# Attention re-laid on 128 partitions, with token tiles of two batches and one set of small steps for three tiles

## The chip, the cores and the metric

The kernel runs on one core of a Trainium2 chip. The metric is device time in microseconds (us) of one launch. A kernel's runs mostly agree within 0.3%. On the chip that most experiments shared, the kernel before itself varied from 1040.6 to 1052.7 us, so the intervals of the ratios are about 0.6% wide to each side, and the smaller differences are read from the traces.

## The reference

The program is an attention without softmax, followed by a balanced mixture of experts. Cut to what matters (B = 8 batches, H = 8 heads, S = 576 tokens, D = 64, all fp32; E = 8 experts):

```python
kv  = np.einsum('bhsd,bhse->bhde', k, v)
out = np.einsum('bhsd,bhde->bhse', q, kv)
rms = np.sqrt(np.mean(out * out, axis=-1, keepdims=True) + 1e-06)
x   = (out / rms * g_norm)            # then (B,H,S,D) -> (B*S, H*D) = 4608 x 512
logits = x @ w_gate                   # 4608 x 8
# all logits from the highest down: a token goes to that expert if neither is taken or full
# (every expert takes 4608 / 8 = 576 tokens); then for each expert:
out[mask] = np.maximum(x[mask] @ w1[e], 0.0) @ w2[e]
```

The gate needs the logits of all tokens, so the assignment cannot start before the attention has ended. That makes the program three stages in a row: attention, assignment, experts.

## The kernel before

The attention stage is the part that the change touches. k and v of a batch lie on 96 partitions of six tokens each, q of a batch's first 512 tokens on 128 partitions of four tokens; the other 64 tokens of two batches share a tile (the "q tail"). A tile of 128 tokens goes through transposes (`qt_ps`, `qt`), the product with the block-diagonal k-v matrices (`o_ps`), squares, a root and its Newton step, and two multiplications out of PSUM: `x_sb` and, for the gate's logits, `part`.

```python
def load_kv(b):
    for name, src in (("k", k), ("v", v)):
        t = att.tile([KP, H, KR, D], FT, name=f"{name}_sb", tag=name)      # KP = 96, KR = 6
        nc.sync.dma_start(t.rearrange("p h j d -> p h (j d)"),
                          src[b].rearrange("h (p j) d -> p h (j d)", j=KR))
        loaded[name, b] = t

def load_q(b):
    t = att.tile([P, H, J, D], FT, name="q_sb", tag="q")                   # J = 4
    nc.sync.dma_start(t.rearrange("p h j d -> p h (j d)"),
                      q[b, :, 0:G, :].rearrange("h (p j) d -> p h (j d)", j=J))
# ... [cut: constants, bd = the block-diagonal matrices]
def kv_product(b):
    for h in range(H):
        ls = slice((h % 2) * D, (h % 2 + 1) * D)
        for j in range(KR):
            nc.tensor.matmul(kv_ps[ls, h // 2, :], lhsT=k_sb[:, h, j, :], rhs=v_sb[:, h, j, :],
                             start=(j == 0), stop=(j == KR - 1))
    nc.vector.tensor_copy(bd[0:D, b, :, 0:D], kv_ps[0:D])
    nc.scalar.copy(bd[D:P, b, :, D:P], kv_ps[D:P])
    # ... [cut: transposes and the gate's columns of bd]

def token_tile(c, rows, batches, x_row):
    # ... [cut: transposes, qt by ScalarE and VectorE in turn, o_ps]
    nc.scalar.activation(sq, o_v, ACT.Square)
    nc.vector.reduce_sum(out=ms, in_=sq.rearrange("p r (l d) -> p (r l) d", l=2), axis=AXX)
    # ... [cut: seven small steps on 128x8, among them one root on ScalarE]
    nc.vector.tensor_tensor(x_row..., o_v..., inv_h.to_broadcast([P, NP, 2, D]), op=AL.mult)
    nc.vector.tensor_tensor(part, o_ps[:, :, P:W]..., inv_h.to_broadcast([P, NP, 2, E]), op=AL.mult)
    nc.vector.reduce_sum(out=lg[:, :, c], in_=part..., axis=AXX)

for b in range(B):
    kv_product(b)
    # ... [cut: q_rows copies on GpSimd; four token tiles; x written by GpSimd's queue]
    if b + 2 < B:
        load_kv(b + 2); load_q(b + 2)
    if b == B - 3: load_w(0)
    if b == B - 2: load_w(1)
# ... [cut: four tiles of q tails, the last x writes]
```

## Time and profile before

| | before |
|---|---|
| time | 1049.75 us (1048.55 to 1050.27, 3 runs) |
| first k-v product | 14.36 us |
| first token tile (first `o_ps`) | 26.74 us |
| end of the attention stage (start of `ones_b`, the first instruction of the assignment) | 186.7 us (the sum of the prediction takes 187.2, the start of GpSimd's `row_id`) |
| DMA rate in the attention, to 130 us | mostly 220 to 290 GB/s |

How to read it: the page gives each engine's busy share in 40 slices, and the three stages can be seen in it with the naked eye. As the change edits the attention alone, the number to follow is the time at which the first instruction of the assignment starts. It can be found in VectorE's list as the instruction that writes `ones_b`, or in GpSimd's as `row_id`; both wait for the last write of x.

### The profile page before, as it was taken

Reading aid. Unit: us, or ns where it says so; the run is one execution under the profiler, and the core shown is the slowest. Engines: PE = TensorE matmul, PEld = TensorE weight load, DVE = VectorE, ACT = ScalarE, POOL = GpSimd, SP = SyncE. Lnnn points to the kernel's source line nnn. Section 1 sums busy time; section 2 is a strip of 40 time slices with the busy share of each in tenths; the row PEclk is TensorE's granted clock in tenths of the full one; section 3 lists DMA queues with packets and bytes.
Section 4 is the critical chain, followed back from the end, with each engine's and each line's share of the span. In section 5 each row is a group of like instructions: output and inputs, shape, how many; then the busy total and the mean of one; then the engine's idle time right before and its main releaser. Section 6 shows DMA issues by size and latency. Waiting matters only on the chain.

```text
span 1045.8 us, 12692 instructions
## 1 busy us (share of the span) xinstructions
PE 756.9 (72%) x5277; PEld 509.7 (49%) x5277; DVE 363.2 (35%) x1295; ACT 98.7 (9%) x212; POOL 105.1 (10%) x132
## 2 busy tenths in 40 slices
PE   3796884223223223216999999999999999999996
PEld 3786874122212222213755747557466475574752
DVE  0666576565675666674110101101011011010100
ACT  1332231000000000000110101101001011010100
POOL 2211110000000000004120110210202100101001
PEclk9998796555555555555999999999999999999999
DMA  9999991000000000003133212330323122301000
GB/s 225 261 259 295 268 385 60 22 1 1 1 1 2 1 1 1 2 1 89 47 146 106 105 62 86 138 112 25 133 96 136 44 72 101 105 1 41 6 20 25
DMA packets 45721, 91.01 MB, mean 87 GB/s; under 512 B 7008, under 2 KB 27488, under 8 KB 44640
## 3 DMA queue, kind: packets, MB, share of 16 engines
q1 hardware_dynamic: 37632, 61.87, 20.8%
q0 software_dynamic: 7328, 28.32, 7.5%
q8 instruction: 41, 0.67, 0.3%
q10 hardware_dynamic: 704, 0.02, 0.1%
q14 instruction: 16, 0.13, 0.0%
HBM read 71.32 MB, written 18.87 MB: 86 GB/s over the span
## 4 chain that ended last, share of the span: by engine, by line
issue 50%; DVE 22%; PE 18%; POOL 6%; DMA 2%; ACT 2%; POOLq 0%; SPq 0%; DVEq 0%; ACTq 0%
PE n_ps L318 6%; PE o_ps L158 4%; DVE over L313 4%; POOL out_dram L523 4%; PE kv_ps L129 3%; POOL xg L482 2%; DVE cand L311 2%; DMA v_sb<-in_v_dram 1%; DVE up L328 1%; DVE step L308 1%; DVE hi L330 1%; PE qt_ps L147 1%; DVE lo L332 1%; PE k_ps L326 1%; DVE full L321 1%
## 5 line engine op out<-in xcount | busy, mean ns | idle before, releaser
L519 PE MATMUL y_ps<-w_sb,hid 128*128 128x512 f32 (+1 forms) x640 | 280.2, 594 | 0.0
L509 PE MATMUL h_ps<-xt,w_sb 128*128 128x288 f32 x1024 | 251.7, 408 | 0.0
L509 PEld LDWEIGHTS h_ps<-xt,w_sb 128*128 128x128 f32 x1024 | 194.5, 191 | 58.8 <-issue 5.7
L519 PEld LDWEIGHTS y_ps<-w_sb,hid 128*128 128x128 f32 (+1 forms) x640 | 112.5, 179 | 151.3 <-issue 150.7
L318 PE MATMUL n_ps<-best,over 128*16 128x8 bf16 x2016 | 62.5, 176 | 146.1 <-DVE over L313 105.5
L318 PEld LDWEIGHTS <-over 128*16 128x16 bf16 x2016 | 57.0, 89 | 173.9 <-DVE over L313 172.2
L471 DVE TENSOR_SCALAR hid<-h_ps 128x288 f32<-128x288 f32 x64 | 29.3, 458 | 253.2 <-PE h_ps L509 253.2
L475 DVE COPY y_sb<-y_ps 128x512 f32<-128x512 f32 (+1 forms) x17 | 11.8, 691 | 208.7 <-PE y_ps L519 208.7
L482 POOL DMA_INDIRECT xg<-x_dram,ids x40 | 37.9, 946 | 450.1 <-DVE ids L448 295.7
L158 PE MATMUL o_ps<-bd,qt 128*128 128x144 f32 (+1 forms) x320 | 54.9, 361 | 25.3 <-DVE rt L173 19.7
L523 POOL DMA_INDIRECT out_dram<-y_sb,ids x40 | 38.5, 964 | 323.6 <-ACT y_sb L469 189.4
L158 PEld LDWEIGHTS o_ps<-bd,qt 128*128 128x128 f32 (+1 forms) x320 | 49.2, 232 | 28.1 <-issue 24.7
L129 PE MATMUL kv_ps<-v_sb,k_sb 96*64 96x64 f32 x768 | 44.2, 242 | 14.4 <-DMA v_sb<-in_v_dram 14.4
L129 PEld LDWEIGHTS kv_ps<-v_sb,k_sb 96*64 96x64 f32 x768 | 41.4, 152 | 17.9 <-issue 16.2
L465 ACT ACTIVATE hid<-h_ps 128x288 f32<-128x288 f32 x64 | 26.3, 411 | 221.9 <-PE h_ps L509 221.9
L313 DVE TENSOR_TENSOR over<-mx,cand 128x576 bf16<-128x576 f32 x56 | 42.3, 755 | 1.5
L467 ACT ACTIVATE xt<-t_ps,g_col 128x512 f32<-128x512 f32 (+1 forms) x17 | 11.5, 675 | 326.3 <-DMA xg<-x_dram,ids 311.5
L469 ACT COPY y_sb<-y_ps 128x512 f32<-128x512 f32 (+1 forms) x23 | 13.4, 584 | 253.6 <-PE y_ps L519 253.6
L321 DVE SCALAR_TENSOR_TENSOR full<-n_ps,goal 16x8 f32<-16x8 f32 x56 | 8.6, 153 | 67.3 <-PE n_ps L318 67.3
L164 DVE TENSOR_REDUCE ms<-sq 128x8 f32<-128x512 f32 x36 | 24.6, 685 | 19.8 <-ACT sq L162 19.3
L162 ACT ACTIVATE sq<-o_ps 128x512 f32<-128x512 f32 x36 | 21.5, 597 | 73.1 <-PE o_ps L158 73.1
L473 DVE TENSOR_SCALAR xt<-t_ps,g_col 128x512 f32<-128x512 f32 (+1 forms) x23 | 15.4, 669 | 35.8 <-PE t_ps L493 33.8
(143 smaller groups left out, 471.6 us busy)
## 6 DMA issues: line engine op xcount, KB each, us to landing
w_sb<-in_moe_w_dram SPq DMA_DIRECT2D x16, 2048.0 KB, 9.7
k_sb<-in_k_dram SPq DMA_DIRECT2D x8, 1152.0 KB, 13.2
v_sb<-in_v_dram SPq DMA_DIRECT2D x8, 1152.0 KB, 18.1
q_sb<-in_q_dram SPq DMA_DIRECT2D x8, 1024.0 KB, 18.7
x_dram<-x_sb POOLq DMA_DIRECT2D x8, 1024.0 KB, 8.9
q_tail<-in_q_dram SPq DMA_DIRECT2D x8, 128.0 KB, 6.3
x_dram<-x_sb POOLq DMA_DIRECT2D x2, 512.0 KB, 5.4
xg<-x_dram,ids POOLq DMA_INDIRECT x40, 6.2
```

Of the source, the lines that this page charges most:

```text
L129: nc.tensor.matmul(kv_ps[ls, h // 2, :], lhsT=k_sb[:, h, j, :], rhs=v_sb[:, h, j, :], start=(j == 0), stop=(j == KR - 1))
L158: nc.tensor.matmul(o_ps[ps_, r, 0:W], lhsT=qt[:, r, ps_], rhs=bd[:, b, r], start=True, stop=True)
L162: nc.scalar.activation(sq, o_v, ACT.Square)
L164: nc.vector.reduce_sum(out=ms, in_=sq.rearrange("p r (l d) -> p (r l) d", l=2), axis=AXX)
L313: nc.vector.tensor_tensor(over, mx.rearrange("p (c o) -> p c o", o=1).to_broadcast([P, GC, NCAND]), cand.rearrange("p (o n) -> p o n", o=1 ...
L318: nc.tensor.matmul(n_ps, lhsT=over[:, c, :], rhs=best[:, :, c], start=(c == 0), stop=(c == GC - 1))
L465: nc.scalar.activation(dst, src, ACT.Relu)
L471: nc.vector.tensor_scalar(dst, in0=src, scalar1=0.0, scalar2=None, op0=AL.max)
L482: nc.gpsimd.indirect_dma_start(out=xg[0:nr, :], out_offset=None, in_=x_dram, in_offset=bass.IndirectOffsetOnAxis(ap=ids[0:nr, e * NB + n:e ...
L509: nc.tensor.matmul(h_ps, lhsT=w1[:, d, f * P:(f + 1) * P], rhs=xt[:, d, cs], start=(d == 0), stop=(d == DC - 1))
L519: nc.tensor.matmul(y_ps[0:nr, :], lhsT=hid[:, f, a:a + nr], rhs=w2[:, f, :], start=(f == 0), stop=(f == FC - 1))
L523: put = nc.gpsimd.indirect_dma_start(out=out, out_offset=bass.IndirectOffsetOnAxis(ap=ids[0:nr, e * NB + n:e * NB + n + 1], axis=0), in_=y ...
```

## The change

The intent: transfers in longer runs on all partitions; less work for VectorE; tiles that need no tail.

- k and v: 128 partitions of nine tokens (half a head pair each). The k-v product becomes 72 matmuls on two quarters of the array that lie diagonally to one another.
- q: a tile is 64 tokens of each of two batches. Each batch's q goes to 64 partitions: the even batch's to the lower half by SyncE's queue, the odd batch's to the upper half by GpSimd's.
- The small steps are done once for three tiles, on 24 columns. `o_ps` is copied out of PSUM by ScalarE, the multiplication for x goes to GpSimd, all `qt` copies go to VectorE.
- The first two experts' weights are loaded behind all of q, k and v; x is written by SyncE's queue.

```diff
-            t = att.tile([KP, H, KR, D], FT, name=f"{name}_sb", tag=name)
+            t = att.tile([P, NP, R, D], FT, name=f"{name}_sb", tag=name)
             nc.sync.dma_start(
-                t.rearrange("p h j d -> p h (j d)"), src[b].rearrange("h (p j) d -> p h (j d)", j=KR)
-            )
+                t.rearrange("p r j d -> p r (j d)"),
+                src[b].rearrange("h s d -> (h s) d").rearrange("(r p j) d -> p r (j d)", r=NP, j=R))
-    def load_q(b):
-        t = att.tile([P, H, J, D], FT, name="q_sb", tag="q")
-        nc.sync.dma_start(
-            t.rearrange("p h j d -> p h (j d)"), q[b, :, 0:G, :].rearrange("h (p j) d -> p h (j d)", j=J)
-        )
+    def load_q(i):
+        t = att.tile([P, H, R, D], FT, name="q_sb", tag="q")
+        for n, eng in enumerate((nc.sync, nc.gpsimd)):
+            eng.dma_start(t[n * HP:(n + 1) * HP].rearrange("p h j d -> p h (j d)"),
+                          q[2 * i + n].rearrange("h (p j) d -> p h (j d)", j=R))
     # [cut: order of the loads: k0, v0, q0, k1, v1]
-        for h in range(H):
-            ls = slice((h % 2) * D, (h % 2 + 1) * D)
-            for j in range(KR):
-                nc.tensor.matmul(kv_ps[ls, h // 2, :], lhsT=k_sb[:, h, j, :], rhs=v_sb[:, h, j, :],
-                                 start=(j == 0), stop=(j == KR - 1))
+        for r in range(NP):
+            for j in range(R):
+                for l in range(2):
+                    ls = slice(l * D, (l + 1) * D)
+                    nc.tensor.matmul(kv_ps[ls, r, :], lhsT=k_sb[ls, r, j, :], rhs=v_sb[ls, r, j, :],
+                                     start=(j == 0), stop=(j == R - 1))
     # [cut: token_group replaces token_tile; in it, for each of three tiles]
+                for n in range(2):
+                    ps_ = slice(n * HP, (n + 1) * HP)
+                    nc.tensor.matmul(o_ps[ps_, r, 0:W], lhsT=qt[:, r, ps_], rhs=bd[:, 2 * i + n, r],
+                                     start=True, stop=True)
+            nc.scalar.activation(sq..., o_ps[:, :, 0:P], ACT.Square, scale=D ** -0.5)
+            nc.scalar.copy(o_sb[:, t], o_ps[:, :, 0:W])
+            nc.vector.reduce_sum(out=ms[:, t * H:(t + 1) * H], in_=sq..., axis=AXX)
     # [cut: root, reciprocal and three fused small steps on 24 columns]
+        nc.gpsimd.tensor_tensor(x_sb..., o_sb...[:, :, 0:P]..., inv...to_broadcast(...), op=AL.mult)
+        nc.vector.tensor_tensor(part, o_sb...[:, :, P:W]..., inv...to_broadcast(...), op=AL.mult)
+        nc.vector.reduce_sum(out=lg[:, :, c:c + T]..., in_=part..., axis=AXX)
+        nc.sync.dma_start(x_dram[...][:, j0:j0 + T], x_sb.rearrange("p (t f) -> p t f", t=T))
```

## The prediction

> **What bounds the kernel now.** I began with the page: the share of each engine by slice says that the program has three stages (a slice is 26.1 us).
>
> ```profile
> PE   3796884223223223216999999999999999999996
> PEclk9998796555555555555999999999999999999999
> DMA  9999991000000000003133212330323122301000
> GB/s 225 261 259 295 268 385 60 22 1 1 1 1 2 1 1 1 2 1 89 47 146 106 105 62 86 138 112 25 133 96 136 44 72 101 105 1 41 6 20 25
> ```
>
> Slices 1 to 7 are the attention, 8 to 18 the assignment at half clock, the rest the experts. The change edits the attention and two lines of the assignment's setup; so it can only move the time at which the assignment starts. Everything after that is a serial chain which I carry over unchanged. Next, the chain that ended last, in order of time, shows where the stage begins and ends:
>
> ```profile
> 1.20 13.03 DMA v_sb<-in_v_dram
> 14.36 7.03 PE kv_ps L129 x96
> ...
> 26.74 3.91 PE o_ps L158 x16
> ...
> 156.72 3.87 PE o_ps L158 x16
> ...
> 163.96 3.64 PE o_ps L158 x32
> ...
> 179.92 6.46 DMA x_dram<-x_sb
> 188.45 0.46 PE end_ps L262
> ```
>
> First products at 14.36 us, first token tile at 26.7, last write to memory lands at 186.4, and the waits say that VectorE's first instruction of the assignment waited 7.3 us for it. **The stage is 187 us.** To about 155 us it is held by the transfers: in windows of 5 us from 5 to 155 us the DMA share is 0.80 to 1.18 at mostly 220 to 290 GB/s, and only the windows with expert weights and x writes (130 to 155 us) reach 388 to 424. The last 32 us (155 to 187) have no loads: they are the last tiles and their chain. So bytes per second are poor exactly for q, k and v. The trace's DMA records say why: a packet of 2048 bytes takes 84 ns in the median and one of 4096 takes 159 (24 to 26 bytes per ns), q's 1024 take 53, but the 1536-byte packets of k and v, which fill 96 partitions, take 112 on average (13.7 bytes per ns), with a spread from 65 to 145.
>
> **What the Trainium skill says.**
> (1) "SBUF — State Buffer", Door 1: the DMA port swizzle: a transfer is as fast as the share of the 16 ports that its partitions reach; by its table partitions 0 to 95 load eight ports fully and eight by half. The spread of 65 to 145 ns agrees; k and v on 128 partitions should lose it. It also says that 64 partitions reach eight ports, which applies to each half of the new q load.
> (2) "TensorE: Matmul & The Clock Gate", Part 3 (row/col tiling): matmuls on different tiles of the array run at once. The trace agrees for column tiles: at half clock 16 records of full-width o_ps take 3.87 us (242 ns each), 32 records of 64 columns 3.64 us (114 each, partly warm), with starts in pairs. No run shows it for tiles that differ in row and column, as the new k-v product needs.
> (3) "SBUF — State Buffer", two separate sides: GpSimd and VectorE share a port pair as an exclusive lock, which VectorE needs for two SBUF inputs or a two-port mode. The trace agrees: one TENSOR_SCALAR, 0.17 us else, is held until GpSimd's copies end at 48.06.
>
> ```profile
> 45.78 2.28 POOL L199 COPY q_rows<-q_sb 128x512 f32<-128x512 f32 x4
> ...
> 46.89 1.20 DVE L165 TENSOR_SCALAR ms<-ms 128x8 f32<-128x8 f32 x1
> ...
> 48.71 0.17 DVE L165 TENSOR_SCALAR ms<-ms 128x8 f32<-128x8 f32 x1
> ```
>
> (4) "GPSIMD Engine Reference", 3.1: a two-input fp32 op of 2048 elements takes 4497 ns there. No GpSimd op of this trace has two inputs; its one-input copies of 512 take 616 ns.
>
> **The change part by part.**
> *Loads.* q, k, v are 28.3 MB still, now in 2304-byte runs. Estimate from the 2048-byte packets: 84 + 256/26 = 94 ns, 12,288 packets on 16 engines = 72 us, where the before's k, v, q and q-tail packets add up to 86 + 31 + 6 = 123 us. Minus 51 us of transfers, and the 8.4 MB of weights (some 21 us) now queue behind all of q, k and v. The transfers cease to bound: a pair of batches needs 7.1 MB and 2.4 MB of x, about 25 us at 380 GB/s.
>
> *TensorE.* o_ps: 16 half-width records per tile instead of 8, in pairs: 0.98 us warm either way. Transposes stay. k-v product: 72 matmuls a batch instead of 48, that is 144 records; if the two halves pair up, 72 x 57 ns (the warm start-to-start distance of the old records) = 4.1 us; if not, 8.2. The old took about 4.7 warm. TensorE per pair of batches: 8.2 + 9 x 0.98 + 9 x 0.52 + 2 x (0.45 + 1.08) = 25 us.
>
> *VectorE.* x's multiplication (36 x 0.69 = 25 us) goes to GpSimd, the seven small steps become four per three tiles, all qt copies come to it. Sum: 36 x 0.69 + 36 x 0.685 + 12 x (0.8 small + 0.35 part + 0.4 sum) + 8 x 0.64 = 73 us against about 123 before.
>
> *ScalarE.* A copy of 576 elements per tile (about 0.65 us, from 0.60 for 512) is added, 36 of them; half of the qt copies leave: 55 us against 47. Not a bound.
>
> *GpSimd.* 12 copies of 1536 (3 x 0.614 = 1.84 us) and 12 two-input multiplications of 1536 (estimate from the skill's row: 3.4 us). 63 us in all, not a bound by itself, **but each multiplication holds the shared port.** The order of instructions puts one reduction (0.69 us) between the new inverse and the gate's product `part`, which has two SBUF inputs. GpSimd gets the inverse first, so `part` waits 3.4 - 0.7 = 2.7 us, with every later qt copy behind it. The last group of a pair has no reduction there and should slip in ahead of GpSimd.
>
> *The path, per pair of batches* (both k-v products must be done before its first tile, and the order puts the next pair's first kv copy behind the whole VectorE tail of this pair). From VectorE free to the first tile's o_ps: 0.42 copy + 0.45 + 0.59 + 1.08 + 62 matmuls of the second product 3.5 + 0.42 + transposes 0.95 + 0.59 + 1.08 + 0.22 + 0.98 = 10.3 us. From there VectorE: 7 qt copies 4.8 + 9 sums 6.2 + small 2.4 + part 1.05 + gate sums 1.2 = 15.7, two lock waits 5.4, some 3 us of latency for squares and roots. **34.5 us a pair.**
>
> *Sum.* Start: k0, v0 and GpSimd's half of q0 (3.5 MB) land near 12.5 us, k1, v1 near 25 (8.3 MB with what runs beside them), second product to 29.5, first o_ps at 34. First pair done at 34 + 24 = 58; two pairs more: 127; the fourth up to its last inverse, some 31 us: 158; x multiplication 3.4, write about 4.5 (1024 KB took 8.9 before, this is 768 KB from the faster queue): 166. Setup of row ids: two VectorE ops, 0.37 us less. The assignment starts at 166 instead of 187.2: 1049.75 - 21.5 = **1028 us**.
>
> **The rivals.**
> *A: the lock costs nothing* (the gate's product gets ahead, or the multiplication takes 2 us). Then a pair takes about 28 us, TensorE is the bound, the start falls near 148: 1010 us. For it: 51 us of transfers do leave. Against it: the held instructions above.
> *B: the products don't pair, or the clock halves in the waits.* The old trace ran cold in all windows with such waits (clock 0.61 to 0.71 at 100 to 110 us); 3 to 4 us a pair, start at 178: 1040 us.
> *C: x writes wait behind 8.4 MB of weights on one queue.* Weights are issued right behind the last k and v, near 100 us, and land near 128; the third pair's x writes stand behind them, and with two x buffers its third multiplication waits some 5 us. The fourth pair's come later; hidden, unless loads end much later than I think.
> *D: transfers stay the bound*, at 260 GB/s: 36 MB are 138 us before the last pair's tiles: no gain. The 388 to 424 GB/s of the weights speak against it.
>
> **Range and chances.** The middle is 1028, almost on the line of 2% (1028.8). A and B are about equally likely departures and span 1010 to 1042; I take 1011 to 1042 as the range. Slower would need both products unpaired and the writes stuck: 0.03. Faster by over 2%: 0.52; within 2%: 0.45.
>
> **What would show it.** Right: DMA idle at times before 100 us and packets near 94 ns; `part` lasting about 3 us in two groups of three; GpSimd's multiplication near 3.4 us; k-v records starting in pairs, 57 ns apart; the first assignment instruction near 166. Wrong: `part` at 0.35 us (A), k-v records 57 ns one after the other (B), the SP queue waiting to issue x (C), DMA share at 1 until the end (D). It fails too if the experts' stage changes, which I take as equal.

## More of the kernel before

The DMA view of the first 190 us in slices of 4.75 us shows the stage's transfers, in GB/s, before:

```profile
GB/s 143 227 243 276 232 264 267 229 273 243 272 330 230 298 239 218 286 331 258 233 393 237 222 223 230 292 314 399 410 420 389 409 286 0 0 221 0 1 204 20
```

This row will be compared with that of other kernels: near 250 while q, k and v are loaded, near 400 where the experts' weights are.

## The result

The changed kernel takes **1035.03 us** (1033.59 to 1035.96, 4 runs) against 1050.01 us of the kernel before in the same rounds: a ratio of 0.9875 by the record, with a 95% interval of 0.9841 to 0.9908. (The two medians give 0.9857, which lies in that interval.) That is 1.2 to 1.4% faster, thus within 2%, and inside the predicted range; the predicted time, 1028, was 7 us too low.

The page after, busy tenths in 40 slices as before:

```profile
PE   1888882322322322317999999999999999999996
PEclk9899996555555555556999999999999999999998
DMA  9998982000000000004032312321223112301000
GB/s 221 297 240 278 320 331 110 1 2 1 1 1 1 2 1 1 1 1 137 24 135 97 137 35 83 147 107 67 91 97 138 65 52 103 107 0 41 6 20 25
```

The assignment and the experts look as they did: from the assignment's first instruction to the end of the profiled run it is 860.2 us, where it was 859.1. TensorE is idle in the first slice now (a 1 where there was a 3) and busy at 8 through the rest of the attention; the DMA row is still at 8 and 9 up to 155 us, although the transfers were to be 51 us shorter. The DMA view of the first 190 us, in slices of 4.75 us:

```profile
GB/s 165 223 241 250 235 184 350 390 304 189 329 237 211 259 258 173 384 379 243 333 94 287 341 294 193 339 404 395 399 395 403 226 169 160 5 169 166 0 3 0
```

There are now slices at 340 to 390 GB/s, but between them ones below 260, and the first 30 us are among the slowest of all. Lines of the chain that ended last, in order of time (start, duration, what):

```profile
6.86 29.55 DMA v_sb<-in_v_dram
36.45 7.08 PE kv_ps L131 x144
...
47.85 2.10 PE o_ps L162 x28
...
57.44 2.53 DVE part L182
...
73.42 3.76 PE kv_ps L131 x124
...
170.60 3.24 DMA x_dram<-x_sb
```

The chain now starts with a transfer of v that takes until 36 us; the first product of batch 1 starts at 36.45, and the first full token tile at 47.85 (first `o_ps` of all: 45.04). Later, `part` appears in the chain, 2.5 us long. Two groups of the stage show why (line, engine, operation, shapes, count; busy us, mean ns of one; idle before and what ended it):

```profile
L177 POOL TENSOR_TENSOR x_sb<-o_sb,inv 128x1536 f32<-128x1536 f32 x12 | 33.2, 2769 | 41.6 <-DVE inv L175 32.4 <-ACT o_sb L166 6.0 <-issue 2.2
...
L182 DVE TENSOR_TENSOR part<-o_sb,inv 128x192 f32<-128x192 f32 x12 | 19.6, 1631 | 0.2
```

`part` is 192 elements wide and takes 1.63 us in the mean. Single ones take 2.2 to 2.7 us (seven of the twelve), or 0.36; the long ones are those that start while GpSimd's multiplication runs, and they end with it. The first of them, from the lists of GpSimd and of VectorE:

```profile
57.00 2.76 POOL L177 TENSOR_TENSOR x_sb<-o_sb,inv 128x1536 f32<-128x1536 f32 x1 [6.88 <-DVE inv L175]
...
57.36 2.61 DVE L182 TENSOR_TENSOR part<-o_sb,inv 128x192 f32<-128x192 f32 x1
```

This is the wait at the shared port that the prediction had named; below it is called the lock.

The DMA records of the stage, by size of packet, add up as follows (mean duration; sum over all, divided by 16 engines):

| | before | after |
|---|---|---|
| k and v | 12,288 x 1536 B, 112 ns: 86 us | 8,192 x 2304 B, part of the row below |
| q | 8,192 x 1024 B, 60 ns: 31 us; 4,096 x 256 B: 6 us | SyncE's half 2,048 x 2304 B |
| all of 2304 B | | 10,240, 130 ns: **83 us** |
| GpSimd's half of q | | 1,024 x 4608 B, 327 ns: **21 us** |
| sum | 123 us | **104 us** (72 us were predicted) |

Where k and v run alone, their packets take 98 to 99 ns in the mean and the rate is 377 to 390 GB/s, near the 94 ns and 380 GB/s of the prediction. Where SyncE's half of q runs alone, its packets take 198 to 199 ns in the median and the rate is 184 to 194 GB/s. GpSimd's larger packets take some 300 ns beside k and v.

### The profile page after: what moved, and what is told of

Read it like the earlier page. It is cut to its first block, busy times and chain, and to the rows that moved or that the text cites. A ratio compares the mean times of both kernels' runs of the same rounds, so it can differ in the third digit from the quotient of the medians. Undisturbed runs are those within 1.5% of the kernel's fastest.

```text
span 1034.2 us, 13718 instructions
## 1 busy us (share of the span) xinstructions
PE 750.4 (73%) x5917; PEld 499.6 (48%) x5917; DVE 341.8 (33%) x1060; ACT 104.1 (10%) x206; POOL 135.2 (13%) x117
## 4 chain that ended last, share of the span: by engine, by line
issue 49%; DVE 23%; PE 15%; POOL 7%; DMA 4%; ACT 1%; POOLq 0%; DVEq 0%; ACTq 0%
PE n_ps L310 6%; DVE over L305 4%; POOL out_dram L510 4%; DMA v_sb<-in_v_dram 3%; PE o_ps L162 3%; PE kv_ps L131 3%; POOL xg L469 2%; DVE cand L303 2%; DVE part L182 2%; DVE up L320 1%; DVE step L300 1%; DVE hi L322 1%; DVE lo L324 1%; PE qt_ps L155 1%; DVE full L313 1%
## 5 line engine op out<-in xcount | busy, mean ns | idle before, releaser
L131 PE MATMUL kv_ps<-v_sb,k_sb 64*64 64x64 f32 x1152 | 45.0, 240 | 27.5 <-DMA v_sb<-in_v_dram 25.9
L131 PEld LDWEIGHTS kv_ps<-v_sb,k_sb 64*64 64x64 f32 x1152 | 42.1, 154 | 30.8 <-issue 27.3
L162 PE MATMUL o_ps<-bd,qt 128*64 128x144 f32 x576 | 46.6, 304 | 10.9 <-DVE qt L157 8.9
L162 PEld LDWEIGHTS o_ps<-bd,qt 128*64 128x64 f32 x576 | 38.4, 144 | 15.0 <-ACT o_sb L166 8.8
L454 ACT ACTIVATE xt<-t_ps,g_col 128x512 f32<-128x512 f32 (+1 forms) x17 | 11.5, 675 | 324.0 <-PE t_ps L480 321.8
L177 POOL TENSOR_TENSOR x_sb<-o_sb,inv 128x1536 f32<-128x1536 f32 x12 | 33.2, 2769 | 41.6 <-DVE inv L175 32.4
L480 PEld LDWEIGHTS t_ps<-ident,xg 128*128 128x128 f32 (+1 forms) x160 | 18.7, 149 | 17.9 <-issue 8.0
## 6 DMA issues: line engine op xcount, KB each, us to landing
q_sb<-in_q_dram SPq DMA_DIRECT2D x4, 1152.0 KB, 17.3
```

The lines of the kernel that those rows point to most:

```text
L131: nc.tensor.matmul(kv_ps[ls, r, :], lhsT=k_sb[ls, r, j, :], rhs=v_sb[ls, r, j, :], start=(j == 0), stop=(j == R - 1))
L162: nc.tensor.matmul(o_ps[ps_, r, 0:W], lhsT=qt[:, r, ps_], rhs=bd[:, 2 * i + n, r], start=True, stop=True)
L177: nc.gpsimd.tensor_tensor(x_sb.rearrange("p (a l d) -> p a l d", l=2, d=D), o_sb.rearrange("p t r w -> p (t r) w")[:, :, 0:P].rearrange("p ...
```

## The experiments

Twelve kernels ran; each gave the right result. Stage ends are the start of the assignment's first instruction, as above. Some edits hold the first experts' weights back with a one-column copy into their tile, since the scheduler would otherwise move them ahead of loads of k and v; that is said where it is so. The scheduler also sets the order of TensorE's instructions, so an edit of the loads can move them; five experiments (e6 to e9 and e13) suffer from that, and perhaps e12.

### 1. Is the lock the bound? (e1_part_first)

```diff
-        nc.gpsimd.tensor_tensor(x_sb..., op=AL.mult)
         nc.vector.tensor_tensor(part, ..., op=AL.mult)
         nc.vector.reduce_sum(out=lg[...], in_=part..., axis=AXX)
+        nc.gpsimd.tensor_copy(x_sb[:, 0:1], part[:, 0, 0, 0:1])   # GpSimd waits for part
+        nc.gpsimd.tensor_tensor(x_sb..., op=AL.mult)
```

> The changed kernel, but GpSimd's multiplication of a group waits until VectorE has done that group's gate product (a one-element copy out of it, ahead of the multiplication). Theory (the shared port is on the path): the gate product takes 0.36 us in all 12 groups instead of 2.3 to 2.7 in 8 of them, VectorE is free some 4 us sooner in each pair of batches, the distance between first k-v copies of successive pairs falls from 32.2 us to about 28, the assignment starts near 160 instead of 174: 1021 us. Rival (TensorE's own chain is the bound, VectorE's waits are hidden): the distance stays at 31 to 32 us, 1033 to 1037 us.

Measured: 1035.29 us (1034.26 to 1037.03), ratio to before 0.9881 (0.9820 to 0.9942), the same as the change itself. The mechanism worked: `part` took 0.35 us everywhere, and the first k-v copies of the second and third pair came at 67.76 and 97.95 us instead of 70.16 and 102.41. But then TensorE stopped in the middle of the next product. TensorE's list (start, duration; in brackets the idle time before):

```profile
101.13 2.19 PE L131 MATMUL kv_ps<-v_sb,k_sb 64*64 64x64 f32 x67
106.59 2.97 PE L131 MATMUL kv_ps<-v_sb,k_sb 64*64 64x64 f32 x57 [3.27 <-issue]
```

and the list of SyncE's queue, which issues the loads:

```profile
97.35 0.38 SPq L74 DMA_DIRECT2D k_sb<-in_k_dram  x1
100.61 0.32 SPq L189 DMA_DIRECT2D x_dram<-x_sb  x1
101.02 0.39 SPq L74 DMA_DIRECT2D v_sb<-in_v_dram  x1
```

A load of v stood in the queue behind an x write, and this one waited for GpSimd's multiplication, which this edit had made later. The copy of the second product came at 109.60 us, against 109.47 in the changed kernel: what the lock had cost came back as a wait for v. So the lock is real, but not alone on the path; TensorE's trace calls the wait "issue", and only the queue's own list shows what it was.

### 2. The same, from the other side (e5_mult_vector)

```diff
-        nc.gpsimd.tensor_tensor(x_sb..., op=AL.mult)
+        nc.vector.tensor_tensor(x_sb..., op=AL.mult)
```

> The changed kernel with the multiplication of x on VectorE instead of GpSimd. Theory (GpSimd's multiplication costs VectorE through the lock about what it saves it): VectorE gains 12 x 1.7 us of work and loses 12 x 1.3 us of waits, last multiplication 1.7 us instead of 2.8: 1031 to 1039 us. Rival (taking the multiplication off VectorE was a gain of the change): 1043 us or more.

Measured: 1032.70 us (1032.03 to 1033.23), ratio 0.9859 (0.9799 to 0.9920), stage end 170.75. One group of VectorE's list:

```profile
56.08 1.75 DVE L177 TENSOR_TENSOR x_sb<-o_sb,inv 128x1536 f32<-128x1536 f32 x1
57.74 0.35 DVE L182 TENSOR_TENSOR part<-o_sb,inv 128x192 f32<-128x192 f32 x1
```

VectorE does in 1.75 us what GpSimd does in 2.77, so 2.1 us for both steps replace a `part` held for 2.5. To hand this work to GpSimd freed VectorE of next to nothing in the two groups of three where the lock holds it.

### 3. The layout of k and v alone (e4_before_kv)

The kernel before with only the new `load_kv` and `kv_product`; q, the tiles, the small steps and the weights stay.

> The kernel before with one part of the change alone: k and v on 128 partitions of nine rows, and the k-v product on two quarters of the array. Theory: packets of k and v take 94 to 99 ns instead of 112 on average and are 8192 instead of 12288, 37 us less of transfers; TensorE, busy for 129 of the first 180 us, then is the next bound, so the stage shortens by 15 to 25 us: 1025 to 1035 us. Rival (k and v's layout is worth little, the gain came from the q layout, the three-tile steps or GpSimd): 1045 us or more.

Measured: **1027.47 us** (1026.25 to 1028.34), ratio 0.9813 (0.9752 to 0.9873). TensorE's list and VectorE's first instruction of the assignment, in this kernel:

```profile
11.32 5.79 PE L129 MATMUL kv_ps<-v_sb,k_sb 64*64 64x64 f32 x144 [11.32 <-DMA v_sb<-in_v_dram]
...
23.61 2.23 PE L158 MATMUL o_ps<-bd,qt 128*128 128x144 f32 x16
```

```profile
163.63 0.17 DVE L240 MEMSET ones_b<- 128x128 bf16 x1 [7.24 <-DMA x_dram<-x_sb]
```

The stage ends at 163.6 us, 23.1 sooner than before and 10.4 sooner than after. The packets of k and v take 105 ns in the mean, 54 us of 16 engines instead of 86. So this one part of the change is worth more than the whole, and **the other parts together lose about as much as 10 us of the stage**. The first token tile is there at 23.6 us here, at 45.0 in the changed kernel: the loss sits at the start, and about half of it is won back later.

### 4. Both halves of q on one queue (e2_q_on_sp)

```diff
-        for n, eng in enumerate((nc.sync, nc.gpsimd)):
+        for n, eng in enumerate((nc.sync, nc.sync)):
-    load_kv(0); load_q(0); load_kv(1)
+    load_kv(0); load_kv(1); load_q(0)
```

> The changed kernel, but both halves of q go on the same queue as k and v, behind k and v of the first two batches. Theory (GpSimd's half of q, with packets of 4608 bytes to 64 partitions, takes bandwidth from the first k and v): v of batch 0 lands near 9 us instead of 22.6, of batch 1 near 15 instead of 36.4, q of the first pair near 28, first full token tile near 31 instead of 47.8. Each half of q alone should show packets near 200 ns (half the ports), so a pair needs about 31 us of transfers, close to the 32 us that it takes: part of the gain may be lost again, 1019 to 1030 us. Rival (the start is limited by the memory and not by the queue's order): first tile not before 42 us, 1033 us or more.

Measured: 1049.43 us (1047.40 to 1051.58), ratio 1.0027 (0.9964 to 1.0089): the whole gain is gone, and the theory's 1019 to 1030 us were missed. The start was indeed early (first product at 11.4 us, first `o_ps` at 34.3), but the pairs were 38 to 41 us apart and the stage ended at 185.4. The DMA view, as before in slices of 4.75 us:

```profile
GB/s 166 293 385 241 203 207 327 248 207 200 252 379 233 240 107 327 207 203 256 403 259 242 0 215 304 205 202 352 402 394 396 400 396 256 169 0 166 147 186 2
```

In one queue the transfers don't mix, so each shows its own rate: 385 for k and v, **200 to 207 for a half of q**. In this kernel q takes as long as k and v together, with half their bytes.

### 5. The second half of q on another queue (e9_q_half_act)

```diff
-        for n, eng in enumerate((nc.sync, nc.gpsimd)):
+        for n, eng in enumerate((nc.sync, nc.scalar)):
```

(with the weights held back). It asks whether GpSimd's packets of 4608 bytes are to blame, or the 64 partitions.

> The changed kernel with one edit of substance: the second half of q moves from GpSimd's queue to ScalarE's (the weights are held back by a small copy so that they keep their place). Packets of q should then be of 2304 bytes on both queues. Theory (GpSimd's packets of 4608 bytes are what slows k and v at the start): v0 lands by 16 us, v1 by 30, first tile near 38 instead of 45; the later pairs stay tied to SyncE's queue; 1026 to 1032 us. Rival (half of the ports for q, not the packet size): first kv at 20 us or later, first tile over 42 us, 1033 to 1038 us.

Measured: 1045.90 us (1040.71 to 1050.08), ratio 0.9999 (0.9934 to 1.0064), slower than both expectations; the stage ended at 178.8. The packets of ScalarE's queue were of 2304 bytes and took 137 ns in the mean, with k's and v's at 128 to 141 beside them. The first product started at 16.2 us instead of 22.6, as the theory said, but the second at 36.48 us against 36.45 of the changed kernel: SyncE's own half of q ran after v0, at 183 ns a packet and 199 GB/s, and took away what had been won. So the size of GpSimd's packets decides who has the larger share at first, but not when all of the first pair is there; my theory of the moment fell. Beyond that the run is muddied: the scheduler had put ten matmuls of batch 2's product ahead of the first full tile, and they waited for v until 47.6 us.

### 6. Loads uncoupled from the multiplication (e6_x_pool, e7_x_pool_part, e8_q_act)

In e6 x is written by GpSimd's queue (with the weights held back), in e7 the multiplication is behind `part` as well, and in e8 both halves of q go to ScalarE's queue as well, with k0, v0, k1 and v1 alone on SyncE's:

```diff
-        nc.sync.dma_start(x_dram[...], x_sb...)              # e6, e7, e8
+        nc.gpsimd.dma_start(x_dram[...], x_sb...)
+        nc.gpsimd.tensor_copy(x_sb[:, 0:1], part[:, 0, 0, 0:1])   # e7, e8: ahead of the multiplication
-        for n, eng in enumerate((nc.sync, nc.gpsimd)):       # e8
+        for n, eng in enumerate((nc.scalar, nc.scalar)):
```

> The changed kernel with its x writes on GpSimd's queue, so that no load of k or v stands behind an x write on SyncE's queue (the first two experts' weights are held back by a small copy until the last pair's k-v product, so that they don't move ahead of the loads). Theory (loads are coupled to the last multiplication through SyncE's queue): loads come earlier, but the start (first tile near 45 us) and the lock stay, so VectorE's tail becomes the only bound: pairs stay near 32 us apart; stage end 172 to 175, 1031 to 1036 us. Rival (the queue's order is itself what sets the 32 us): pairs about 29 us apart, stage end near 165, near 1026 us. Against both: GpSimd's own cost of issuing eats it, over 1038 us.

> The run before with, in addition, GpSimd's multiplication held until the gate's product is done (no lock wait). Theory (lock and queue order are about equally long, and both must go): part 0.35 us everywhere, no wait for v between the first and the fourth pair, first k-v copies of the pairs near 67.8, 98 and 128 us, stage end near 165, 1024 to 1028 us. Rival (the loads' rate is the bound, whatever the queue): the third pair's first copy near 109 + 26 = 135 us as in the changed kernel, no gain, 1033 to 1037 us.

> The run before with, in addition, both halves of q on ScalarE's queue behind its small loads, and k0, v0, k1, v1 alone on SyncE's queue: no packets of 4608 bytes from GpSimd beside k and v. Theory (the late start is the share that GpSimd's large q packets take from k and v): first k-v product by 13 us, second by 26, first tile near 32 instead of 45 us, stage end near 153, 1010 to 1016 us. Rival (the bytes needed ahead of the first tile set it, whoever carries them): first tile after 40 us, 1020 to 1028 us.

Measured: e6 1041.53 us (1040.42 to 1046.57), ratio 0.9957 (0.9890 to 1.0024), stage end 178.2; e7 1038.83 (1037.61 to 1039.02), 0.9915 (0.9854 to 0.9976), 175.4; e8 1037.71 (1035.58 to 1038.53), 0.9905 (0.9843 to 0.9968), 174.5. None reached what its theory said. In each the loads were still late with SyncE's queue free of x writes. In e6 and e7, too, the scheduler had put the first ten matmuls of batch 6's product ahead of the third pair's tiles, since the loads now came earlier in its order; they waited for v until 115.1 us in e6 and 110.8 in e7, and the tiles with them. That wait was 1.6 and 3.6 us long, so it is not all of the loss. The weights that were held back were a second difference: they landed until 175.4, 172.6 and 172.0 us (148.7 in the changed kernel), beside the last x writes. And e6 took what its third guess said, over 1038 us from GpSimd's own cost of issuing; no run tells that apart from the order. So these three say little on the queue's order, and why they are slow stays open. In e8 the transfers had a queue to each kind, and the DMA view says what the common limit was:

```profile
GB/s 164 289 320 274 279 275 280 276 274 281 275 278 271 305 311 207 335 368 188 311 258 328 392 209 239 12 168 61 235 45 158 377 394 410 408 388 134 0 3 0
```

From 14 to 62 us, ten slices in a row lie between 271 and 281 GB/s: a ceiling, as long as a half of q and k or v are on their way together. One account, which is an estimate, fits it and the other kernels. Let a transfer into 64 neighbouring partitions be able to use half of the ports, at no more than the 207 GB/s that experiment 4 showed. In e8 packets of q and of k or v, 2304 bytes each, alternate; so that half carries q's share and half of the other's, 3/4 of all bytes, and the total can be no more than an estimated 207 / 0.75 = 276. In the changed kernel GpSimd's packets have 4608 bytes against 2304; the half carries 5/6 of all, an estimated 207 / 0.833 = 248: its slices between 9 and 24 us show 241, 250 and 235. "DMA: Bandwidth & Descriptors", section "Queues, rings and completion order", of the Trainium skill says that a DMA engine takes turns between the queues that have work for it, a packet at a time. Its packet can hold several descriptors (single copies), so it need not be one packet of the trace; both estimates assume one of the trace's packets a turn. The records agree: between 10 and 20 us the changed kernel started 355 packets of GpSimd's and 360 of SyncE's, so GpSimd's half had 164 GB/s, and k and v 83.

### 7. q at all ports, and nothing else (e10_q_interleaved)

If the ports are the cause, it is enough to change the partitions in which a half of q lies. Even and odd partitions instead of lower and upper ones reach all ports with the same 64 partitions, bytes and queues. The transposed tile then has the two batches in alternate columns, and the matmuls pick them with a step of two:

```diff
-            eng.dma_start(t[n * HP:(n + 1) * HP].rearrange("p h j d -> p h (j d)"),
+            eng.dma_start(t[n::2].rearrange("p h j d -> p h (j d)"),
...
-                    nc.tensor.matmul(o_ps[ps_, r, 0:W], lhsT=qt[:, r, ps_], rhs=bd[:, 2 * i + n, r],
+                    nc.tensor.matmul(o_ps[ps_, r, 0:W], lhsT=qt[:, r, n::2], rhs=bd[:, 2 * i + n, r],
```

> The changed kernel with q's two halves in even and odd partitions instead of the lower and upper 64 (and the matmuls of o_ps taking every second column of qt); same queues, same order, same bytes. Theory (q on 64 neighbouring partitions reaches half of the ports: its 18.9 MB for all of q, k and v cost 104 us of the 16 engines instead of the 72 that the prediction counted, and the k and v packets beside it suffer): q packets of 2304 bytes near 97 ns instead of 190, GpSimd's of 4608 near 180 instead of 327; v0 there by 16 us, first tile near 34 instead of 45, pairs 30 to 32 us apart, stage end near 162, 1019 to 1025 us. Rival (two transfers of 64 partitions each stay slow however the partitions lie, or GpSimd's packet size takes the share): first tile over 41 us, 1031 to 1037 us. Against both: the strided weights of o_ps load slower, o_ps above 46.6 us in all.

(The 18.9 MB in this text are k and v alone; q, k and v together are 28.3 MB. The 104 us are those of all three.)

Measured: **1025.71 us** (1024.68 to 1026.06), ratio 0.9800 (0.9748 to 0.9851). TensorE's list at the start of the changed kernel:

```profile
22.61 7.17 PE L131 MATMUL kv_ps<-v_sb,k_sb 64*64 64x64 f32 x144 [22.61 <-DMA v_sb<-in_v_dram]
36.45 7.08 PE L131 MATMUL kv_ps<-v_sb,k_sb 64*64 64x64 f32 x144 [3.31 <-DMA v_sb<-in_v_dram]
45.04 0.46 PE L162 MATMUL o_ps<-bd,qt 128*64 128x144 f32 x2
```

and of this one:

```profile
17.31 6.04 PE L131 MATMUL kv_ps<-v_sb,k_sb 64*64 64x64 f32 x144 [17.31 <-DMA v_sb<-in_v_dram]
27.52 5.96 PE L131 MATMUL kv_ps<-v_sb,k_sb 64*64 64x64 f32 x144 [0.79 <-DMA v_sb<-in_v_dram]
34.98 0.46 PE L162 MATMUL o_ps<-bd,qt 128*64 128x144 f32 x2
```

The first tile comes 10.1 us sooner. The DMA view of this kernel:

```profile
GB/s 164 282 389 381 391 377 396 331 380 149 148 269 169 210 386 402 386 203 61 176 373 405 393 403 395 393 403 392 298 169 0 166 2 224 109 0 3 0 3 0
```

From 9 to 33 us the loads run at 377 to 396 GB/s. GpSimd's packets take 194 ns in the mean instead of 327, all of 2304 bytes 101 instead of 130; together 77 us of 16 engines instead of 104. The first instruction of the assignment, in the changed kernel and here:

```profile
174.02 0.17 DVE L232 MEMSET ones_b<- 128x128 bf16 x1 [5.53 <-DMA x_dram<-x_sb]
```

```profile
163.52 0.17 DVE L232 MEMSET ones_b<- 128x128 bf16 x1 [5.51 <-DMA x_dram<-x_sb]
```

The stage ends 10.5 us sooner, about as much as the first tile comes sooner. Up to there the instructions of every engine and of SyncE's queue stand in the same order in both, and the strided weights cost nothing (`o_ps` 46.7 us busy in all, 46.6 before the edit). Thus **q's place in 64 neighbouring partitions is shown as the cause of the late start**. That it acts through the ports is the reading of the prediction's point (1); the rates fit it, but no run shows the ports themselves. The k and v packets still have to share with GpSimd's larger ones (v0 at 17.3 us, 11.4 where q stood behind in the same queue), which is a smaller matter.

One more comparison is worth making. With q spread over even and odd partitions the whole change ends the stage at 163.5 us, and k's and v's layout alone (e4) ended it at 163.6. From the first `o_ps` to the stage's end it is 128.5 us here and 140.0 in e4: the other parts of the change shorten the work after the start by 11.5 us. But the first `o_ps` comes at 35.0 us here and at 23.6 in e4, so the start takes 11.4 us more: the first product begins 6 us later (17.3 against 11.3), and a tile of two batches then needs the second product too (27.5). The two cancel, and what each of the other parts brings alone was not tried.

### 8. With the ports free, does the lock count? (e11_q_int_part)

The edits of experiments 7 and 1 together.

> The run before with, in addition, GpSimd's multiplication held until the gate's product is done, as in the earlier run of that kind. Theory (without q's half ports the loads are ahead of the work, so what the lock takes now counts): pairs 28 to 29 us apart without a wait for v, stage end 150 to 154, 1010 to 1015 us. Rival (x writes ahead of the loads in SyncE's queue still bind): a wait for v in the second or third pair, stage end 158 to 163, 1019 to 1025 us.

Measured: **1021.76 us** (1018.21 to 1027.71), ratio 0.9769 (0.9699 to 0.9839), stage end 160.4: the fastest of all kernels, in the range of its rival expectation. The first two pairs are 30.2 us apart (56.27, 86.47), two less than with the lock. In the third there is the wait of experiment 1 again. SyncE's queue:

```profile
86.04 0.38 SPq L74 DMA_DIRECT2D k_sb<-in_k_dram  x1
89.13 0.32 SPq L189 DMA_DIRECT2D x_dram<-x_sb  x1
89.54 0.39 SPq L74 DMA_DIRECT2D v_sb<-in_v_dram  x1
```

and TensorE:

```profile
95.11 3.25 PE L131 MATMUL kv_ps<-v_sb,k_sb 64*64 64x64 f32 x57 [3.26 <-issue]
```

The load waits for the x write ahead of it, which waits for the multiplication (ended at 89.1 us). This is a matter of order in the queue, not of rate: in most slices from 9 to 47 us the rate is 380 to 395 GB/s now.

### 9. Two further combinations (e12_q_int_sp, e13_q_int_x_pool)

e12 is e11 with both halves of q on SyncE's queue behind k0, v0, k1, v1. e13 is e11 with the x writes on GpSimd's queue and the weights held back. It was run on another chip.

> The run before with, in addition, both halves of q on SyncE's queue, behind k0, v0, k1 and v1. Theory (at full ports the order of the bytes alone sets the start: v0 at 11.5 us, v1 near 18, q near 24): first tile near 30 us, pairs 28 to 29 us apart, stage end 146 to 150, 1006 to 1011 us. Rival (one queue in order, with q in it, waits for the multiplications too): pairs 30 us or more apart, 1015 us or more.

> All three together: q in even and odd partitions, GpSimd's multiplication behind the gate's product, and the x writes on GpSimd's queue (the first two experts' weights held back until the last pair's k-v product). Theory (with q at all ports, the wait for v in the third pair of the run with the first two edits comes from loads that stand behind x writes in SyncE's queue): no wait for v after the first pair, first k-v copies of the pairs near 56.3, 86.5 and 116.5 us, stage end 152 to 155, 1012 to 1016 us. Rival (x writes of GpSimd's queue land late beside loads or weights, and GpSimd's order holds up q_rows): stage end 160 or later, 1021 us or more.

Measured: e12 1037.67 us (1036.99 to 1038.64), ratio 0.9919 (0.9866 to 0.9971), stage end 175.0; e13 1026.71 (1025.11 to 1028.12), 0.9822 (0.9796 to 0.9847), stage end 165.1. Both fell in the range of their rival expectations. e12 started as its theory said, with the first `o_ps` at 29.0 us, and gives the cleanest comparison for the ports. With all loads in one queue, as in experiment 4, the DMA view is:

```profile
GB/s 169 287 387 390 391 391 393 389 200 166 137 281 0 178 367 395 391 191 126 340 15 3 219 404 392 395 407 387 401 394 410 112 169 0 166 167 166 0 3 0
```

Between 9 and 38 us q moves like k and v, at 387 to 393 GB/s (391 from 17 to 24 us, which is q alone by the order of the queue), against 200 to 207 when it went to neighbouring partitions. But the pairs lie 39 us apart. The transfers stand still at times, and TensorE is partly idle at a clock of 0.72 between 50 and 70 us; the scheduler had put the second product of a pair (144 records at 60.67 us) behind first tiles and transposes, where the changed kernel has it right behind the first. In e13 there was the order of e6 and e7 again: ten matmuls of batch 6's product stand ahead of the third pair's tiles and waited for v until 100.76 us, and the last x writes went out beside the weights held back (one took 7.4 us). I read both as costs of the order, but no run isolates it from what the rivals named (x writes and loads in one queue, or late x writes), so for these two kernels the cause stays open.

## Why the prediction was right or wrong

**Which end of the stage.** Predicted 166, measured 174.0; the total was 7 us too low, the stage 8. The terms, in us (e10 is the run with q at all ports):

| step of the sum | predicted | changed kernel | e10 |
|---|---|---|---|
| first `o_ps` | 34 | **45.0** | 35.0 |
| to the second pair's first k-v copy | 24 | 25.1 | 25.1 |
| two pairs | 69 | 64.9 | 65.0 |
| to the last inverse | 31 | 32.4 | 32.0 |
| multiplication, write, start | 8 | 6.5 | 6.5 |
| stage end | 166 | **174.0** | 163.5 |

**The step that failed is the transfers' term**: "84 + 256/26 = 94 ns, 12,288 packets on 16 engines = 72 us", and with it "first o_ps at 34". The 94 ns are right for k and v, and were carried over to q, whose halves fill 64 neighbouring partitions; there a 2304-byte packet took 190 to 200 ns, GpSimd's 4608 bytes 327, and the sum was 104 us. The text had the fact in its hands: point (1) cites that 64 partitions reach eight ports "which applies to each half of the new q load", and the sum then didn't apply it. With that one term repaired in the kernel (e10), the first tile came at 35.0 us, the engines' sum was 77 us, and the kernel took 1025.71 us where 1028 had been predicted. So the 11 us at the start are the miss; some 4 us were given back by pairs that were shorter than predicted, so that part of the total's nearness is luck.

**"The transfers cease to bound."** Wrong in the changed kernel: its first 36 us are one wait for v. Rival D, "transfers stay the bound", had this part right, though at the start and in no way "until the end". After the start the loads were close behind VectorE's tail: when e1 shortened the tail, a wait for v of 3.3 us took its place. The reading of the old trace was also a little off: not only the windows from 130 to 155 us passed 388 GB/s, but also that from 95 to 100 (392), in which x writes and the end of a q ran.

**The lock.** Right in its mechanism and nearly in its size: `part` took 2.2 to 2.7 us in seven of the eight groups where it was to wait (the text of e1 counts eight) and 0.36 in the last group of a pair; GpSimd's multiplication 2.77 us where 3.4 had been estimated. What was not foreseen is that to remove the wait is worth nothing as long as loads stand behind x writes in SyncE's queue (e1), and only some 3 to 4 us with fast loads (e11 against e10: 163.5 to 160.4).

**The pairing of the k-v matmuls.** Right: 124 records in 3.76 us, thus 61 ns to a pair, where 57 was said. Rival B fell, apart from the first two products, with 7.2 and 7.1 us for 144 records. For the second the trace's granted clock was 0.58; for the first it shows no lower clock, as its clock records begin only at 28.7 us.

**The path of a pair.** 34.5 predicted, 32.4 measured. The sum is right as a sum; which of its terms were 2 us too long, beside the shorter wait at the lock (some 2.1 us each where 2.7 were taken), was not broken down.

**Rival C.** Right, and hidden as it said, but mis-sized: the third pair's x writes stood behind the weights, the first of them landed at 150.6 us, and the pair's last multiplication ran at 150.8, 16.6 us after its inverse was there (some 5 us were estimated). It had no effect on the end.

**The last write.** 3.2 us for 768 KB where 4.5 was estimated.

**The probabilities.** The outcome fell in "within 2%", which had 0.45; the larger share, 0.52, lay on "faster by over 2%". The working behind the middle, 1028, had the first tile 11 us too early.

## What to carry to other kernels

Count a transfer by what its own partitions reach, not by the rate of its neighbour: a load into the lower or the upper 64 partitions cost here as much time as one of twice the bytes into all 128, and slowed whatever shared the engines with it. Two batches can share a tile just as well in even and odd partitions, with a step of two in the matmul's weights, at no cost that this trace shows. Before taking a lock or a wait off one engine, look at what the next queue in line waits for: an in-order queue that carries both the results and the loads ties the next load to the last result.

## What the Trainium skill lacked or had wrong

- "SBUF — State Buffer", Door 1 and the section on two DMAs for the two halves: the page concludes that all 16 ports need one transfer across all 128 partitions, and advises 32 over 64 partitions otherwise. Its port table would allow for it, but it doesn't say that 64 partitions with a step of two reach the full rate: 391 GB/s for q in e12, against 200 to 207 into 64 neighbouring ones in e2 (its own 196 for such a transfer agrees).
- The same page says nothing of what a half-port transfer does to a full one beside it: with packets of equal size the total stayed at 271 to 281 GB/s (e8), with packets of 4608 against 2304 bytes at 235 to 250 (changed kernel), far below the 377 to 390 of k and v alone.
- "DMA: Bandwidth & Descriptors" gives the size of a packet in general (a number of descriptors, and for GpSimd's path preferably at most 4096 B), but not by queue. The same kind of copy went out in packets of 4608 bytes from GpSimd's queue and of 2304 from SyncE's and ScalarE's, which gave GpSimd's twice the bytes per turn: 164 against 83 GB/s.
- "GPSIMD Engine Reference", 3.1: the two-input figure scaled to 1536 elements gives an estimate of 3.4 us; 2.77 us were measured, with one input broadcast in rows of 64.
- "TensorEngine Tiling (Array Packing)", Gotcha 1, says that row tiles cannot use the same PSUM bank at a time. Here the two row tiles of the k-v product wrote to different partitions of one 1 KB tile per partition, and their records still started 61 ns a pair, with the right result. The two tiles differ in column too, a case that the sentence doesn't tell apart; that their writes met in time is not shown.
